# Storing the weight sums of the seven-product down projection ahead of time, and redistributing additions, query units and output tiles, in an fp32 attention-plus-GLU layer

## The chip, the cores and the metric

The kernel runs on one core of one Trainium2 chip. The metric is the device time of one execution in microseconds (us); three runs give the median. A profiled execution of the same program gives the rows that are read below. PE is the matrix engine, DVE the vector engine, ACT the scalar engine, POOL is GpSimd, and SP is the engine that issues nearly all transfers.

## The reference

Everything is fp32. With S = 2048 tokens, D = 512, 32 heads of 16 and F = 1376:

```python
xn = layernorm(x)
q, k, v = split(xn @ wqkv)                        # 32 heads of 16
phi(t) = [softmax(t @ w_phi), softmax(-t @ w_phi)]  # 32 features of a head
num = phi(q) @ (phi(k).T @ v);  den = phi(q) @ sum(phi(k)) + 1e-6
s = (num / den) @ wo
gate, up = xn @ W_gate, xn @ W_up                 # 512 -> 1376
g = silu((gate * (gate > 0) * up) @ W_down)       # 1376 -> 512
out = x + s * g
```

## The kernel before

An fp32 product is made of three passes on PE: each operand is split into a high part (a copy on ACT, rounded) and a low part (value minus high part, a subtraction on POOL or DVE), and `mm3` adds low times high, high times low and high times high in one PSUM tile. A pass of 128x128 weights over 512 columns is the unit of PE's work. In the names of tiles, an ending h or l (`wth`, `wtl`, `hh`, `hl`) is the high or low part.

The program has three stretches. First come the normalisation, the keys, values and queries, the state `phi(k).T v`, and the splitting of the GLU's weights, which are written back to DRAM (`wspill`, the names `ws` in the trace). Then the GLU runs twice over its eleven blocks `f` of 128 hidden units: the first half for tokens 0 to 1023 (blocks 0 and 1 of 512 tokens), the second half for tokens 1024 to 2047. In each `f`, `gate_up` multiplies gate and up weights (`wa`, `wb`, `wc`, `wd`) by column sets of the normalised tokens in a seven-product form; its PSUM tiles are `pa`, `pb`, `pc`, `pd`, and DVE adds them up (`pb<-pb,t`, `t<-pd,t`, `r<-pd,r` and so on).

In the second half the down projection has a seven-product form too, called turned: the first eight blocks form two groups (`GROUPS`), and each group needs seven products in the order `ORDER = (5, 3, 1, 6, 7, 2, 4)`. Product `i` has a weight operand `AW[i]` (tiles `wth`, `wtl`) and a token operand `OPS[i]`. Of the weight operands 1, 2 and 4 are plain quarters of the group's down weights (`rd`); 5, 6, 3 and 7 are sums of quarters (`ds`). `weights()` makes all seven while the second half runs: a sum, a high part, a low part each. `operand_parts()` makes the token operands by subtractions such as `t<-t,t` and `e<-t,e`. A helper `sooner()` puts each such addition on DVE or POOL, whichever the planner believes free first. `turned_down(g)` issues the products in PSUM tiles `py`, interleaved with `gate_up` at the steps `STEPS_AT`; DVE adds them to `y`.

The queries are worked off in eight units (`UNITS`), of two 256-token pieces each, by `q_pair(u)` and `q_back(u)`: DVE transposes (`pq<-pql`), takes maxima and minima (`mx<-pq`), subtracts (`eq<-pq,mx`), ACT exponentiates, POOL weighs (`ez<-eq,zB`) and normalises (`eq<-eq,qs`), DVE sums (`qs<-eq`, `qs<-ez`) and transposes (`ez<-eq`), PE makes `pnum`, ACT copies it out (`eq<-pnum`), SP stores it. Units 0 to 2 belong to the first half of the GLU and units 3 to 7 to the second.

An output tile of 128 tokens is `s` times `g` plus `x`: `out_tile` multiplies by `wo` (PSUM `pso`, 12 passes), DVE multiplies by the gate, and `sx<-yk,sx` adds `x`. Tokens 1024 to 2047 that fall to `TURNED_Q` use `out_turned`, which transposes back on DVE (`z<-y`) and adds `x` as `z<-z,sx`, half on POOL and half on DVE.

Every engine executes its instructions in program order. That order is partly written out, and partly set by a planner, `Clock`: work that is not on PE's path is held in generators, each step of which names an engine and tiles; `pump()` issues a step when the planner's estimate says that the tiles are there and the engine is at most `LIMIT` ahead (for queries times a factor), and `finish()` forces a generator to its end. The estimates are costs in the code, not measurements. All instructions go through one helper, so that the trace names line 74 for nearly all.

Of the kernel before, what the change touches and what calls it, by code (L numbers as in the profile page):

```python
# [54 lines left out]
SLACK = 3000  # L55
# [119 lines left out]
def layer_kernel(ctx: ExitStack, tc: tile.TileContext, x, wkT, wqT, wv, wo, wf, cst, out):  # L175
# [31 lines left out]
    def f32(t):  # L207
        return t.bitcast(F32)
# [369 lines left out]
    def f_prep(f, keep=True):  # L578


        rg, rd, tab = RAW.pop(f)
        b11, b12, b21, b22 = (rg[c][:, :, s, :] for c in range(2) for s in range(2))
        ta, tb = tab or two("tab", True)
        yield "gpsimd", b22
        add(nc.gpsimd, tb[:, 0], b12, b11, ALU.subtract)
        add(nc.gpsimd, ta[:, 1], b22, b12, ALU.subtract)
        if keep:
            wa, wb = w_pair("wa"), None
        else:
# [36 lines left out]
        put(f, 6, wd)  # L626
        yield from sums_of(ordered(fd[1]), plain(rd), ordered(f32(fd[0])), ALU.subtract, fd[0])
        if f not in IN_GROUP:
            put(f, 8, fd[1])
        if keep:  # L630
            FT[f], WD[f] = [wa, wb, wc, wd], fd
            nxt = f + 1
            while nxt in AHEAD:
                nxt += 1
            del rg, rd, ta, tb, tab
            if nxt < NF and nxt not in RAW:
                f_load(nxt)
        DONE.add(f)
        yield None,
# [69 lines left out]
            WQ.clear()  # L709
        yield  # L710

    RD, MADE = {}, set()

    def halves(t):
        return t.rearrange("p k (a n c) -> p n (k a) c", a=4, n=2)

    def sooner():
        ends = {k: max(pace.free[k], pace.now) + pace.FIXED[k] + pace.RATE[k] * BT for k in ("vector", "gpsimd")}
        return nc.vector if ends["vector"] < ends["gpsimd"] - SLACK else nc.gpsimd

    def d_load(g):
        RD[g] = [u4((P, 2, D), "rd") for h in range(2)]
        for m, f in enumerate(GROUPS[g]):
            nc.sync.dma_start(RD[g][m // 2][:, m % 2, :], wf[f][:, 1024:])

    def weights():

        for g in range(len(GROUPS)):
            d_load(g)
            a11, a21, a12, a22 = (halves(t)[:, x] for t in RD.pop(g) for x in range(2))  # L730
            t = {1: a11, 2: a12, 4: a22}
            for i in ORDER:
                while len(AW) > DEEP:
                    yield 2,
                src = t.pop(i, None)
                if src is None:
                    src = u2((P, 8, 64), "ds")
                    yield "vector", a11, a22
                    add(sooner(), src, *{5: (a21, a22, ALU.add), 7: (a11, a21, ALU.subtract),
                                          3: (a12, t.get(6), ALU.subtract)}[i])  # L740
                AW[i] = [u2((P, 2, 8, 32), f"wt{x}", F32R) for x in "hl"]
                yield "scalar", src
                hi, lo = (t.rearrange("p t k j -> p k t j") for t in AW[i])
                src_ = src.rearrange("p k (t j) -> p k t j", t=2)
                nc.scalar.activation(hi, src_, AF.Copy)
                yield "vector", hi
                add(sooner(), lo, src_, f32(hi), ALU.subtract)
                src_ = hi = lo = None
                MADE.add((g, i))
                if i == 5:  # L750
                    yield "vector", AW[i][1]
                    add(sooner(), src, src, a11, ALU.subtract)
                    t[6] = src
                if i == 7:
                    a11 = a21 = None
            src = a11 = a21 = a12 = a22 = None
        yield None,

    def f_reload(f, part):
# [133 lines left out]
    HS, Y, LATE = {}, {}, []  # L893
    B = {}
    OPS, AW, READY = {}, {}, set()
    queries = operands = making = None

    def raised(f, h1):
        g, block, k = IN_GROUP[f]
# [6 lines left out]
    def operand_parts():  # L906
# [16 lines left out]
        for g in range(len(GROUPS)):  # L923
            for i in ORDER:
                ops, ts = [], []
                for k in range(2):
                    while (g, *needs[i], k) not in B:
                        yield 1,
                    t, a, b = made(g, i, k)
                    if a is not None:  # L930
                        yield "sync", a, b
                        yield "gpsimd", a, b
                        add(sooner(), t, a, b, ALU.subtract)
                    ts.append(t)
                    t = a = b = None
                while len(OPS) > 1:
                    yield 1,
                for k in range(2):
# [9 lines left out]
                    add(sooner(), lo, t, f32(hi), ALU.subtract)  # L948
                    ops.append((hi, lo))
                    del t, hi, lo  # L950
                if i in drops:
# [9 lines left out]
    def turned_down(g):  # L961
# [7 lines left out]
        held = {}  # L969
        for i in ORDER:  # L970
            pace.finish(operands, lambda: (g, i) in READY)
            pace.finish(making, lambda: (g, i) in MADE)
            for t in range(2):
                c = {5: "y", 3: "y", 2: "z"}.get(i, "x"), t
                first = c not in held
                if first:
                    held[c] = ps(name="py")
                p = held[c]
                wh, wl = AW[i]
                mm3(p, lambda k: [x[:, t, 4 * k:4 * k + 4].rearrange("p a j -> p (a j)") for x in (wh, wl)],  # L980
                    lambda k: OPS[i][k], range(2), first)
                del wh, wl
                if t == 1:
# [60 lines left out]
    def q_pair(u):  # L1044
# [34 lines left out]
        late = parts[0][0] in QUERIES[1]  # L1079

        def normalize(j):
            (nc.gpsimd if late else nc.vector).tensor_tensor(
# [103 lines left out]
        yield None,  # L1186

    OHL, OF, SX, YK, LOADED = {}, {}, {}, {}, set()
    yspill = {t: dram((P, D), f"yk{t}") for t in (6, 7)}

    def o_load_turned(n):
        qs = TURNED_Q[n]
# [35 lines left out]
    def out_turned(n, d, w):  # L1228
# [25 lines left out]
    def last_turned():  # L1254
# [28 lines left out]
                nc.scalar.activation(y, y, AF.Silu)  # L1283
        for f in REST_F:
            HS.pop(f), WD.pop(f)
        q = QUERIES[1][-1]
        for n in range(2):
            for d in range(4):
                if n == 1 and d == 1:
                    o_split(q)  # L1290
                out_turned(n, d, WO)
                pace.pump()
                if n == 0 and d == 0:
                    o_split_turned(1)
                if n == 0 and d == 2:
                    o_load(q)
# [467 lines left out]
    def all_queries(half):  # L1764
# [35 lines left out]
    for half in range(2):  # L1800
# [7 lines left out]
        for f in range(NF):  # L1808
# [11 lines left out]
            if f == NF - 1:  # L1820
                if half:
                    o_load_turned(0)
                else:
                    drain()
                    pace.finish(queries)
# [36 lines left out]
        for j, b in enumerate((b1, b0)):  # L1862
            j = 1 - j
            if b == b0:
                for q in QUERIES[half][:2]:
                    o_split(q)
            parts = {}
# [21 lines left out]
        for m, q in enumerate(qs):  # L1889
            if m == 1:  # L1890
                f_reload(1, 0)
            if m + 2 < len(qs):
                o_split(qs[m + 2])
            if m + 4 < len(qs):
# [60 lines left out]
```

## Time and profile before

| what | value |
|---|---|
| median of three runs | 544.26 us (544.08 to 544.73) |
| profiled execution | 544.09 us, span 542.3 us, clock 0.996 |
| PE | 533.2 us busy, 98% of the span, 3162 matmuls |
| DVE | 403.4 us, 74% |
| ACT | 261.1 us, 48% |
| POOL | 398.8 us, 74% |
| transfers | 119.69 MB, mean 221 GB/s |

The profiled execution is 1.79 us longer than its span: what lies around the span. PE is nearly always busy, so the questions are where it stands still, and what lies behind its last matmul. The rows name a tile by the program's name without its number; `x6` in a row of the timeline means six instructions of the same form grouped in one row, and the bracket at its end gives the engine's idle time ahead of the row and what ended it.

### The profile page before, as it was taken

The page shows a single profiled execution, that of the slowest core. Times are in us where ns is not written, and L with a number is a line of the kernel's source. Part 1 is how long each engine was busy: PE and PEld are TensorE (multiplying, and loading weights), DVE is VectorE, ACT ScalarE, POOL GpSimd, SP SyncE. Part 2 cuts the span into 40 slices and gives each one's busy share as a digit, 9 for nine tenths or more (in the row PEclk, how much of TensorE's full clock was granted, in tenths as well). Part 3 has the DMA queues.
Part 4 walks back from the last instruction along what each step waited for, and adds up shares of the span by engine and source line. Part 5 has one row for each costly group of instructions (what it writes and reads, how often), then busy time and mean ns, then how long its engine had stood idle before and what let it go on. Part 6 is the DMA issues. An engine that isn't in the chain of part 4 may idle for free. (4 is left out here: it accounts for less than half of the span.)

```text
span 542.3 us, 9145 instructions
## 1 busy us (share of the span) xinstructions
PE 533.2 (98%) x3162; PEld 435.8 (80%) x3162; DVE 403.4 (74%) x629; ACT 261.1 (48%) x467; POOL 398.8 (74%) x343
## 2 busy tenths in 40 slices
PE   9999999999999999999999999999999999999995
PEld 8898887888887888787888888887787878778784
DVE  5988777687867328789983342899979999799365
ACT  3788757654425565545443250323655452643500
POOL 0669999767788999899896235446799859966652
PEclk9999999999999999999999999999999999999998
DMA  8439789557899646775879996793455456653564
GB/s 271 161 128 331 168 219 241 126 124 184 218 246 354 232 171 222 250 265 216 290 256 342 410 414 266 259 370 108 142 176 196 129 174 215 188 164 95 173 202 131
DMA packets 81166, 119.69 MB, mean 221 GB/s; under 512 B 6880, under 2 KB 39520, under 8 KB 80224
## 3 DMA queue, kind: packets, MB, share of 16 engines
q1 hardware_dynamic: 78960, 111.70, 61.1%
q0 software_dynamic: 2016, 7.34, 7.9%
q8 instruction: 25, 0.41, 0.3%
q14 instruction: 21, 0.17, 0.1%
q10 hardware_dynamic: 144, 0.07, 0.0%
HBM read 66.39 MB, written 48.50 MB: 212 GB/s over the span
## 5 line engine op out<-in xcount | busy, mean ns | idle before, releaser
L74 PE MATMUL pa<-XT,wa 128*128 128x512 f32 x264 | 67.4, 390 | 0.0
L74 DVE TENSOR_TENSOR y<-py,y 128x512 f32<-128x512 f32 x60 | 40.9, 683 | 29.4 <-PE py L74 29.4
L74 PEld LDWEIGHTS pa<-XT,wa 128*128 128x128 f32 x264 | 49.4, 188 | 11.0 <-issue 0.8
L74 POOL TENSOR_TENSOR ez<-eq,zB 128x1024 f32<-128x1024 f32 x16 | 38.4, 2408 | 6.4 <-ACT eq L74 6.4
L74 POOL TENSOR_TENSOR hl<-t,hh 128x512 fp32r<-128x512 f32 x20 | 25.9, 1297 | 15.7 <-ACT hh L74 13.8
L74 PE MATMUL pd<-XT,wd 128*128 128x512 f32 x132 | 33.8, 391 | 0.8 <-DVE t L74 0.7
L74 PE MATMUL py<-fdh,hl 128*128 128x512 f32 x88 | 34.4, 390 | 0.0
L74 PE MATMUL py<-fdl,hh 128*128 128x512 f32 x88 | 34.3, 389 | 0.0
L74 PE MATMUL py<-fdh,hh 128*128 128x512 f32 x88 | 34.2, 389 | 0.0
L74 PE MATMUL pd<-XT,wc 128*128 128x512 f32 x132 | 34.1, 391 | 0.0
L74 PE MATMUL pb<-XT,wb 128*128 128x512 f32 x132 | 33.9, 391 | 0.0
L74 PE MATMUL pc<-XT,wb 128*128 128x512 f32 x132 | 33.8, 390 | 0.0
L74 POOL TENSOR_TENSOR ol<-of,oh 128x512 fp32r<-128x512 f32 (+1 forms) x13 | 19.8, 1548 | 16.9 <-ACT oh L74 13.1
L74 PE MATMUL pq<-XT,wqh 128*128 128x512 f32 (+1 forms) x112 | 30.7, 360 | 0.0
L74 DVE TENSOR_REDUCE mx<-pk 128x32 f32<-128x512 f32 x32 | 20.5, 681 | 13.3 <-PE pk L74 13.3
L74 PE MATMUL pk<-wkh,XT 128*128 128x512 f32 x88 | 30.2, 395 | 0.0
L74 PEld LDWEIGHTS pd<-XT,wd 128*128 128x128 f32 x132 | 24.6, 188 | 6.7 <-DVE t L74 1.6
L74 PEld LDWEIGHTS pb<-XT,wb 128*128 128x128 f32 x132 | 24.6, 188 | 5.9 <-ACT wc L74 0.4
L74 PEld LDWEIGHTS pd<-XT,wc 128*128 128x128 f32 x132 | 24.6, 188 | 5.8 <-issue 0.8
L74 PEld LDWEIGHTS pc<-XT,wb 128*128 128x128 f32 x132 | 24.7, 188 | 5.5 <-issue 0.4
L74 ACT ACTIVATE hh<-t 128x512 fp32r<-128x512 f32 x21 | 13.0, 627 | 30.7 <-DVE t L74 25.6
L74 PE MATMUL pb<-XT,wc 128*128 128x512 f32 x102 | 26.0, 391 | 0.5 <-DVE pb L74 0.5
(252 smaller groups left out, 1607.0 us busy)
## 6 DMA issues: line engine op xcount, KB each, us to landing
xts<-XT SPq DMA_DIRECT2D x4, 1792.0 KB
zacc<-ek POOLq DMA_DIRECT2D x14, 512.0 KB, 5.6
XT<-xts SPq DMA_DIRECT2D x7, 1024.0 KB
rawg<-wf SPq DMA_DIRECT2D x22, 256.0 KB
ws<-wa SPq DMA_DIRECT2D x22, 256.0 KB
ws<-wb SPq DMA_DIRECT2D x22, 256.0 KB
ws<-wc SPq DMA_DIRECT2D x22, 256.0 KB
wa<-ws SPq DMA_DIRECT2D x22, 256.0 KB
```

Of the source, the lines that this page charges most:

```text
L74: return self.tc.keep_in_program_order(op(*a, **k))
```

## The change

- `weight_sums()` is new. It starts with the second query group of the first half's output tiles, makes the four sums of both groups on POOL (`ds`), splits them (`dth` on ACT, `dtl` on POOL), and stores both parts in DRAM (`WDT`). `weights()` makes nothing any more: it fetches the sums from `WDT`, and the plain operands 1, 2, 4 as slices from `wspill`, whose parts 7 and 8 are now stored for all blocks instead of three.
- `sooner()` is gone: the remaining operand additions are always POOL's.
- The `x` addition of the turned tiles is DVE's, but for one half of the first four.
- Unit 3 of the queries moves to the first half (`Q_UNITS`); from unit 3 on the planner's factor for DVE is 0.7, where it was 1.5 from unit 4 on.
- The output tiles of query piece 2 (tokens 512 to 767, tiles 4 and 5) move from the first half's end to the program's end, so that four tiles come last instead of two.
- `d_load(0)` is issued at the last block of the first half; the first half's queries are finished ahead of block 0's last down products, where it was before the last gate and up products.

```diff
-QUERIES = [(0, 1, 2), (6, 7, 4, 5, 3)]
+QUERIES = [(0, 1), (6, 7, 4, 5, 2, 3)]
+Q_UNITS = ((0, 4), (4, 8))
+PLAIN = {1: (0, 0), 2: (0, 1), 4: (1, 1)}
...
-        if f not in IN_GROUP:
-            put(f, 7, fd[0])
+        put(f, 7, fd[0])
...
+    def weight_sums():
+        for g in range(len(GROUPS)):
...
+            t = u2((P, 8, 64), "ds")
+            for i in (5, 6, 3, 7):
...
+                yield "gpsimd", a, b
+                add(nc.gpsimd, t, a, b, op)
+                parts = [u2((P, 2, 8, 32), f"dt{x}", F32R) for x in "hl"]
...
+                yield "scalar", t
+                nc.scalar.activation(hi, src, AF.Copy)
+                yield "gpsimd", hi
+                add(nc.gpsimd, lo, src, f32(hi), ALU.subtract)
+                def put(parts=parts, g=g, i=i):
+                    for x, d in zip(parts, WDT[g, i]):
+                        nc.sync.dma_start(d, f32(x).rearrange("p t k j -> p (t k j)"))
...
     def weights():
...
-                add(sooner(), lo, src_, f32(hi), ALU.subtract)
+                if i in PLAIN:
+                    n, m = PLAIN[i]
+                    AW[i] = [u2((P, 2, 2, P), f"wt{x}", F32R) for x in "hl"]
+                    for k in range(2):
+                        for x, w in enumerate(AW[i]):
+                            nc.sync.dma_start(f32(w[:, k]).rearrange("p t c -> p (t c)"),
+                                              wspill[GROUPS[g][2 * m + k]][7 + x][:, 256 * n:256 * n + 256])
+                else:
+                    yield "sync", *WDT[g, i]
+                    AW[i] = [u2((P, 2, 8, 32), f"wt{x}", F32R) for x in "hl"]
+                    for w, d in zip(AW[i], WDT[g, i]):
+                        nc.sync.dma_start(f32(w).rearrange("p t k j -> p (t k j)"), d)
...
-                        add(sooner(), t, a, b, ALU.subtract)
+                        add(nc.gpsimd, t, a, b, ALU.subtract)
...
-                    add((nc.gpsimd, nc.vector)[h], part, part, SX[n][2 * i + h])
+                    add(nc.vector if n or h else nc.gpsimd, part, part, SX[n][2 * i + h])
...
-        for j in range(2):
-            out_tile(2 * q + j, WO)
-            pace.pump()
+        for q in rest:
+            for j in range(2):
+                out_tile(2 * q + j, WO)
+                pace.pump()
...
-            if parts[0][0] in QUERIES[half]:
-                if u > 3:
-                    yield "limit", (1.5, 1)
+            if u in range(*Q_UNITS[half]):
+                if u > 2:
+                    yield "limit", (0.7, 1)
                 yield from q_pair(u)
```

PE's own order is the same but for two things: the eight `pnum` stand at other places, and the two output tiles (24 passes) stand at the end. The other engines' orders change most in the second half. Three places follow; first the kernel before, then the changed one.

DVE in the second half, where `gate_up` of the fourth and fifth blocks runs. `pb<-pb,t` is the addition that PE's next `pb` products wait for; `qs`, `qr` belong to the queries, `wtl` is a weight operand's low part. Before:

```order
L74 STREAM_TRANSPOSE ez<-eq 128x512
L74 TENSOR_REDUCE qs<-eq 128x64 x2
L74 TENSOR_TENSOR wtl<-ds,wth 128x8x2x32
L74 RECIPROCAL qr<-qs 128x128
L74 TENSOR_REDUCE qs<-ez 128x64
L74 TENSOR_TENSOR wtl<-rd,wth 128x8x2x32
L74 TENSOR_TENSOR pb<-pb,t_4368 128x512
L74 TENSOR_REDUCE qs<-ez 128x64
```

After:

```order
L75 TENSOR_TENSOR r<-pd,r 128x512
L75 TENSOR_REDUCE qs<-eq 128x64 x2
L75 TENSOR_TENSOR pb<-pb,t_4465 128x512
L75 RECIPROCAL qr<-qs 128x128
L75 TENSOR_REDUCE qs<-ez 128x64
L75 TENSOR_TENSOR t_4465<-pd,t_4465 128x512
L75 TENSOR_REDUCE qs<-ez 128x64
L75 SCALAR_TENSOR_TENSOR t_4465<-pb,t_4465 128x512
```

Both low parts have left DVE's order; between `r` and the next `pb` now stand two query sums, where a sum, a reciprocal, a third sum and the two low parts stood besides.

POOL from the first half's output tiles (`ol`, `sx`) into the second half. Before:

```order
L74 TENSOR_TENSOR ol<-of,oh 128x1024 x3
L74 TENSOR_TENSOR sx<-y,sx 128x512 x6
L74 TENSOR_TENSOR ez<-eq,zB 128x1024 x2
L74 TENSOR_TENSOR t_4098<-e_3958,u_3939 128x512
L74 TENSOR_TENSOR t_4112<-e_4049,u_4031 128x512
L74 TENSOR_TENSOR ds<-rd 128x512
L74 TENSOR_TENSOR hl<-t_4098,hh 128x512
L74 TENSOR_TENSOR hl<-t_4112,hh 128x512
L74 TENSOR_TENSOR ds<-ds,rd 128x512
```

After:

```order
L75 TENSOR_TENSOR ol<-of,oh 128x1024 x2
L75 TENSOR_TENSOR sx<-y,sx 128x512 x4
L75 TENSOR_TENSOR ds<-rd 128x512
L75 TENSOR_TENSOR dtl<-ds,dth 128x8x2x32
L75 TENSOR_TENSOR ds<-ds,rd 128x512
L75 TENSOR_TENSOR ez<-eq,zB 128x1024
L75 TENSOR_TENSOR dtl<-ds,dth 128x8x2x32
L75 TENSOR_TENSOR ds<-rd,ds 128x512
L75 TENSOR_TENSOR ez<-eq,zB 128x1024
L75 TENSOR_TENSOR dtl<-ds,dth 128x8x2x32
L75 TENSOR_TENSOR ds<-rd 128x512
L75 TENSOR_TENSOR t_4188<-e_4026,u_4007 128x512
```

The first group's sums now stand ahead of the first operand subtraction `t<-e,u`; their low parts wait for ACT's `dth`.

The program's end, first DVE, then SP. `yk` is an output tile times its gate, `z` a turned tile's. DVE before:

```order
L74 TENSOR_TENSOR z<-z,sx 128x512
L74 STREAM_TRANSPOSE z<-y 128x8x32
L74 TENSOR_TENSOR z<-z,sx 128x512
L74 TENSOR_TENSOR yk<-pso,yk 128x512
L74 TENSOR_TENSOR sx<-yk,sx 128x512
L74 TENSOR_TENSOR yk<-pso,yk 128x4x64
L74 TENSOR_TENSOR sx<-yk,sx 128x256
L74 TENSOR_TENSOR yk<-pso,yk 128x4x64
L74 TENSOR_TENSOR sx<-yk,sx 128x256
```

DVE after:

```order
L75 TENSOR_TENSOR z<-z,sx 128x512 x2
L75 STREAM_TRANSPOSE z<-y 128x8x32
L75 TENSOR_TENSOR z<-z,sx 128x512 x2
L75 TENSOR_TENSOR yk<-pso,yk 128x512 x2
L75 TENSOR_TENSOR sx<-yk,sx 128x512
L75 TENSOR_TENSOR yk<-pso,yk 128x512
L75 TENSOR_TENSOR sx<-yk,sx 128x512
L75 TENSOR_TENSOR yk<-pso,yk 128x4x64
L75 TENSOR_TENSOR sx<-yk,sx 128x256
L75 TENSOR_TENSOR yk<-pso,yk 128x4x64
L75 TENSOR_TENSOR sx<-yk,sx 128x256
```

SP before:

```order
L74 DMA of<-od_5586 128x1024
L74 DMA yk<-yk_167 128x512
L74 DMA yk<-yk_168 128x512
L74 DMA sx<-x 128x512 x2
L74 DMA out<-z 32x8x128 x16
L74 DMA out<-sx 128x512
L74 DMA out<-sx 128x256 x2
```

SP after:

```order
L75 DMA yk<-yk_186 128x512
L75 DMA sx<-x 128x512 x2
L75 DMA out<-z 32x8x128 x4
L75 DMA sx<-x 128x512 x2
L75 DMA out<-z 32x8x128 x12
L75 DMA out<-sx 128x512 x3
L75 DMA out<-sx 128x256 x2
```

Between the last store of a turned tile (`out<-z`) and the last store of all now lie four output tiles on PE instead of two.

More of the change, by code (lines that the diff above doesn't have):

```diff
@@ L710, in q_tile @@
         yield
-    RD, MADE = {}, set()
+    RD, MADE, SUMMED, PUTS = {}, set(), set(), {}
     def halves(t):
         return t.rearrange("p k (a n c) -> p n (k a) c", a=4, n=2)
-    def sooner():
-        ends = {k: max(pace.free[k], pace.now) + pace.FIXED[k] + pace.RATE[k] * BT for k in ("vector", "gpsimd")}
-        return nc.vector if ends["vector"] < ends["gpsimd"] - SLACK else nc.gpsimd
     def d_load(g):
@@ L724, in d_load @@
             nc.sync.dma_start(RD[g][m // 2][:, m % 2, :], wf[f][:, 1024:])
+    WDT = {(g, i): [dram((P, 512), f"wdt{g}{i}{x}") for x in "hl"] for g in range(len(GROUPS)) for i in (5, 6, 3, 7)}
+    def weight_sums():
+        for g in range(len(GROUPS)):
+            if g not in RD:
+                yield 100,
+                d_load(g)
+            a11, a21, a12, a22 = (halves(t)[:, x] for t in RD.pop(g) for x in range(2))
+            yield 40,
+            yield "sync", a11, a22
+            t = u2((P, 8, 64), "ds")
+            for i in (5, 6, 3, 7):
+                a, b, op = {5: (a21, a22, ALU.add), 6: (t, a11, ALU.subtract), 3: (a12, t, ALU.subtract),
+                            7: (a11, a21, ALU.subtract)}[i]
+                yield "gpsimd", a, b
+                add(nc.gpsimd, t, a, b, op)
+                parts = [u2((P, 2, 8, 32), f"dt{x}", F32R) for x in "hl"]
+                hi, lo = (x.rearrange("p t k j -> p k t j") for x in parts)
+                src = t.rearrange("p k (t j) -> p k t j", t=2)
+                yield "sync", t
+                yield "scalar", t
[5 more added lines that the diff above has]
+                        nc.sync.dma_start(d, f32(x).rearrange("p t k j -> p (t k j)"))
+                    SUMMED.add((g, i))
+                PUTS[g, i] = pace.when(parts[1], put)
+                del parts, hi, lo, src, a, b, put
+            del t, a11, a21, a12, a22
+        yield None,
@@ L726, in weights @@
     def weights():
         for g in range(len(GROUPS)):
-            d_load(g)
-            a11, a21, a12, a22 = (halves(t)[:, x] for t in RD.pop(g) for x in range(2))
-            t = {1: a11, 2: a12, 4: a22}
             for i in ORDER:
-                while len(AW) > DEEP:
+                while len(AW) > DEEP or i not in PLAIN and (g, i) not in SUMMED:
                     yield 2,
[L735 to L746, printed above, removed]
-                add(sooner(), lo, src_, f32(hi), ALU.subtract)
-                src_ = hi = lo = None
-                MADE.add((g, i))
[L750 to L755, printed above, removed]
@@ L895, in layer_kernel @@
     OPS, AW, READY = {}, {}, set()
-    queries = operands = making = None
+    queries = operands = making = sums = None
     def raised(f, h1):
@@ L971, in turned_down @@
             pace.finish(operands, lambda: (g, i) in READY)
+            if i not in PLAIN:
+                pace.finish(sums, lambda: (g, i) in PUTS)
+                pace.finish(PUTS[g, i])
             pace.finish(making, lambda: (g, i) in MADE)
@@ L979, in turned_down @@
                 wh, wl = AW[i]
-                mm3(p, lambda k: [x[:, t, 4 * k:4 * k + 4].rearrange("p a j -> p (a j)") for x in (wh, wl)],
+                mm3(p, lambda k: [x[:, k, t] if i in PLAIN else x[:, t, 4 * k:4 * k + 4].rearrange("p a j -> p (a j)")
+                                  for x in (wh, wl)],
                     lambda k: OPS[i][k], range(2), first)
@@ L1077, in total @@
             nc.vector.tensor_reduce(sums[:, s, j, :], src, op=ALU.add, axis=AX.X)
-        late = parts[0][0] in QUERIES[1]
+        late = u > 2
         def normalize(j):
@@ L1824, in layer_kernel @@
                     drain()
-                    pace.finish(queries)
+                    d_load(0)
                     for q in QUERIES[0][:4]:
@@ L1864, in layer_kernel @@
             if b == b0:
+                pace.finish(queries)
+                pace.finish(BACK[Q_UNITS[0][1] - 1])
                 for q in QUERIES[half][:2]:
@@ L1891, in layer_kernel @@
                 f_reload(1, 0)
+                sums = pace.add(weight_sums())
             if m + 2 < len(qs):
```

18 lines of the change are left out of this document (8 added, 10 removed).

## The prediction

> **What bounds the kernel now.** I read four views in this order: the page's engine line, the waits of PE, the work by stretches, and the timeline around each place where PE stood still. The page says that PE is the bound:
>
> ```profile
> PE 533.2 (98%) x3162; PEld 435.8 (80%) x3162; DVE 403.4 (74%) x629; ACT 261.1 (48%) x467; POOL 398.8 (74%) x343
> ```
>
> The change takes no matmul from PE, so it can only win where PE stands still or after its last product. The stretches (start:end, then busy us and count of PE, PEld, DVE, ACT and POOL, then clock, DMA share, GB/s) tell which engine is near its limit beside PE:
>
> ```profile
> 282.00:342.00 60.00, 60.00 (x293) 49.07 (x292) 22.19 (x33) 18.11 (x29) 29.11 (x24) 1.00 0.89 342
> 342.00:471.50 129.50, 127.73 (x641) 102.91 (x639) 119.11 (x163) 59.69 (x99) 96.88 (x63) 1.00 0.59 196
> 471.50:513.00 41.50, 41.32 (x234) 32.38 (x233) 31.89 (x50) 20.08 (x33) 27.14 (x19) 1.00 0.51 157
> ```
>
> DVE is 37% busy in the first half's end, 92% in the body of the second half (119.11 of 129.5), 77% after it. PE loses nothing in the first of these, and its losses fall in the other two. These are the five places, each as the row before the stop and the row after it (the bracket is idle time by a modelled end, so I take starts instead):
>
> ```profile
> 374.14 1.52 PE L74 MATMUL pd<-XT,wc 128*128 128x512 f32 x6
> 376.20 1.65 PE L74 MATMUL pb<-XT,wc 128*128 128x512 f32 x6 [0.53 <-DVE pb L74]
> ...
> 384.93 0.96 PE L74 MATMUL pc<-XT,wb 128*128 128x512 f32 x3
> 386.46 0.47 PE L74 MATMUL py<-XT,wtl 128*128 128x512 f32 x1 [0.58 <-ACT eq L74]
> ...
> 439.28 0.39 PE L74 MATMUL py<-hh,wth 128*128 128x512 f32 x1
> 440.33 1.66 PE L74 MATMUL pd<-XT,wd 128*128 128x512 f32 x6 [0.66 <-DVE t L74]
> ...
> 471.41 0.39 PE L74 MATMUL py<-hh,wth 128*128 128x512 f32 x1
> 471.93 1.67 PE L74 MATMUL pd<-XT,wd 128*128 128x512 f32 x6
> ...
> 480.26 1.52 PE L74 MATMUL pa<-XT,wa 128*128 128x512 f32 x6
> 481.83 0.50 PE L74 MATMUL py<-XT,wtl 128*128 128x512 f32 x1
> ```
>
> Undisturbed, six passes take 1.36 us from start to start (three products of 0.39 us that follow each other at 439.28 and before it start 0.227 apart). So the stops are 376.20 - 374.14 - 1.36 = 0.70; at 386.46, three passes and a slow start of 0.11 after 384.93, 0.74; 440.33 - 439.28 - 0.227 = 0.82; 471.93 - 471.41 - 0.227 = 0.29; 481.83 - 480.26 - 1.36 = 0.21: together 2.76. After each, the first group lasts about 0.11 longer (1.65 against 1.52): 0.55 more. **PE loses 3.31 us in the second half to late operands.** What DVE did just then:
>
> ```profile
> 374.85 0.68 DVE L74 TENSOR_TENSOR eq<-mx,pq 128x512 f32<-128x512 f32 x1
> 375.45 0.69 DVE L74 TENSOR_TENSOR pb<-pb,t 128x512 f32<-128x512 f32 x1
> ...
> 385.62 0.70 DVE L74 TENSOR_TENSOR wtl<-ds,wth 128x512 fp32r<-128x512 f32 x1
> ...
> 439.61 0.67 DVE L74 TENSOR_TENSOR t<-pd,t 128x512 f32<-128x512 f32 x1
> ...
> 469.50 1.78 DVE L74 TENSOR_TENSOR wtl<-rd,wth 128x512 fp32r<-128x512 f32 x1
> 471.20 0.68 DVE L74 TENSOR_TENSOR t<-pd,t 128x512 f32<-128x512 f32 x1
> ```
>
> Each time the operand that PE needs stood in DVE's queue behind something else. At 376.20 it is a query's subtraction, at 471.93 a weight operand of 1.78 us. At 386.46 the profile names ACT, yet the product reads the low part that DVE finished at 386.32, 0.14 us earlier: both were late. At 440.33 no weight work stands ahead, only queries: taking the weight sums alone would not mend that one directly, but the thinner queue may.
>
> The second loss is behind PE's last product:
>
> ```profile
> 532.18 3.50 POOL L74 TENSOR_TENSOR z<-z,sx 128x512 f32<-128x512 f32 x2 [4.88 <-DVE z L74]
> ...
> 534.00 3.95 SPq L74 DMA_DIRECT2D out<-z  x8
> 535.16 1.08 DVE L74 TENSOR_TENSOR sx<-yk,sx 128x512 f32<-128x512 f32 x1
> 536.20 0.28 PE L74 MATMUL pso<-woh,oh 128*128 128x256 f32 x1
> 536.60 0.42 DVE L74 TENSOR_TENSOR sx<-yk,sx 128x256 f32<-128x256 f32 x1
> 537.39 0.43 DVE L74 TENSOR_TENSOR sx<-yk,sx 128x256 f32<-128x256 f32 x1
> 538.05 1.42 SPq L74 DMA_DIRECT2D out<-sx  x3
> ```
>
> SP spends 534.00 to 537.95 issuing eight stores of turned tiles, about 0.49 us apiece, and only then the three of the last tiles, though DVE had the first of them at 536.24. The last is issued about 0.95 us after 538.05, at 539.0, and the span ends at 542.3: 3.3 us from the last issue to the end.
>
> **The change part by part.** Weight sums and low parts, removed from DVE, and a query unit moved (mean ns of one in the groups by shape):
>
> ```profile
> L74 DVE TENSOR_TENSOR wtl<-rd,wth 128x512 fp32r<-128x512 f32 x5 | 7.8, 1566 | 0.1
> L74 DVE TENSOR_TENSOR wtl<-ds,wth 128x512 fp32r<-128x512 f32 x5 | 5.7, 1140 | 0.3
> L74 DVE TENSOR_TENSOR ds<-rd 128x512 f32<-128x512 f32 x3 | 3.9, 1299 | 0.0
> L74 DVE TENSOR_TENSOR ds<-rd,ds 128x512 f32<-128x512 f32 x1 | 2.4, 2410 | 0.8 <-POOL ds L74 0.8
> L74 DVE TENSOR_TENSOR y<-py,y 128x512 f32<-128x512 f32 x60 | 40.9, 683 | 29.4 <-PE py L74 29.4
> L74 POOL TENSOR_TENSOR hl<-t,hh 128x512 fp32r<-128x512 f32 x20 | 25.9, 1297 | 15.7 <-ACT hh L74 13.8 <-DMA pql<-pq 1.8
> L74 DVE STREAM_TRANSPOSE ez<-eq 128x512 f32<-128x512 f32 x32 | 21.2, 686 | 0.1
> L74 DVE TENSOR_REDUCE mx<-pq 128x32 f32<-128x512 f32 x32 | 20.5, 681 | 0.4
> L74 DVE TENSOR_REDUCE qs<-eq 128x64 f32<-128x1024 f32 x16 | 19.1, 1204 | 0.0
> L74 DVE TENSOR_REDUCE qs<-ez 128x64 f32<-128x1024 f32 x16 | 18.9, 1190 | 0.7 <-POOL ez L74 0.7
> ```
>
> The fourteen weight additions on DVE took 7.8 + 5.7 + 3.9 + 2.4 = 19.8 us, all of them in the body of the second half. One of eight query units is at least (21.2 + 20.5 + 19.1 + 18.9) / 8 = 10.0 us by these four groups alone. Without 29.8 us the body has 89.3 us of DVE in 129.5, 69%. That is under the 77% of the stretch after it, where the two smallest stops fall (0.29 + 0.11 and 0.21 + 0.11, 0.72 in all). I take the row nearest to the new load: the stops shrink from 3.31 to 0.7, because queries still stand between `gate_up`'s additions (two sums of 1.2 us ahead of a `pb`, in the listing of the change). The ends are 0 and 3.31: the tighter planner factor can spread the queries so that none is left, or they bunch as they did at 440.33. Gain: 2.6.
>
> DVE's additions with two SBUF inputs (`wtl`, `ds`) take 1.1 to 2.4 us, those that read PSUM (`y`) 0.68, and POOL takes 1.30 for the same shape. The Trainium skill, GPSIMD Engine Reference, section 3.1, has an addition on GpSimd 1.96 times as long as on DVE and keeps to DVE for elementwise work. The trace agrees with that only against the 0.68; against `wtl` and `ds` POOL is no slower. By the page's ratio the move would load POOL with more time than DVE loses, which the rivals take up as a wait; by the rows it is an even exchange.
>
> There were 8 sums and 14 low parts, 14 of these 22 on DVE and 8 on POOL. The six low parts of plain operands vanish, and the other 16 additions are all POOL's: 8 more x 1.30 = 10.4 us. POOL had 96.88 + 27.14 = 124.0 us in the 171 us from 342 to 513; 134.4 would be 79%, before the moved unit's operations are taken off, and the first sums stand right behind the first half's output tiles, where POOL was 49% busy (29.11 of 60). Cost: 0 for PE, covered by that slack; if the cover is gone, the price is that of the third rival.
>
> Transfers: sixteen more stores of 256 KB (parts 7 and 8), sixteen stores and sixteen loads of sums, 24 slices of 128 KB, two gate tiles out and back: about 17 MB, some 9 MB of them in the 129.5 us of the body, 70 GB/s on top of 196. The stretch before ran at 342 GB/s with PE never idle, so I price them at 0. They are 77 more issue rows on SP at about 0.49 us, 38 us over the whole program. Behind a store that waits for POOL's low part stand the next block's weight loads; a wait of a microsecond or two is covered, since they are issued a block ahead of use. Its bounds are 0 and one stop like the largest, 0.93. I take 0.
>
> Unit 3 in the first half: the 10.0 us of DVE and more go where DVE was busy 22.2 of 60 us; PE lost nothing there. The earlier `finish` puts query work ahead of the last down products' additions. Bounds 0 and 0.93; I take 0. The two output tiles move 24 passes, 24 x 0.227 = 5.4 us, from one place on PE to another: 0.
>
> The end: the eight stores of turned tiles now lie four output tiles, 48 x 0.227 = 10.9 us, ahead of PE's end, and SP is free when DVE finishes. DVE's 535.16 row took 1.08 beside the second of POOL's additions, which run to 535.68; alone it should be near 0.68, so that the last pair starts right behind PE's last product: 536.55 + 0.41 + 0.43, about 537.4, issue at 537.45, end 3.3 later at 540.75. Gain 1.55 of 542.3. Ends: 0, if SP is still held, and 1.8.
>
> Sum for the profiled execution: 544.09 - 2.6 - 1.55 = 539.9. The median stands 0.17 above it, so 540.1.
>
> **The rivals.** First, stops remain. Queries stood ahead at 376.20 and 440.33, 1.5 of the 2.76, and four of the second half's five units stay there; a new late operand can replace each old one. Then only the end is won: 544.26 - 1.55 = 542.7. Against it speaks the 23 points of load that DVE loses (92 to 69%). Second, the end is not won: the stores of four tiles' rows queue as before, and only the stops go: 544.26 - 2.6 = 541.7. Against it: ten microseconds of PE lie between. Third, on the slower side: POOL makes every turned operand late. It now makes each sum, each low part and each operand difference in one queue, with `ez<-eq,zB` and the like between. With fourteen products late by x, the time is 539.4 + 14 (x + 0.11); above x = 0.31 it is slower than 545.35. At the 0.58 that PE idled at 386.46 it would be 549.1. For it: POOL's 79%; against: no wait of PE for POOL is among the five. Fourth, all stops go: 539.4. Fifth, the change does little: SP's extra issues delay a block's loads and each of four or five is worth 0.93, which brings back what was won: 543.8 to 544.7.
>
> **How the numbers follow.** A difference under 0.2%, 1.1 us, can't be told from no change here. Chances: forecast with the fourth, 539.0 to 541.2: 0.62, of which 0.05 still lower; first rival 0.15; second 0.10; third 0.08; fifth 0.05. Faster, under 543.2: 0.62 + 0.15 + 0.10 less 0.02 for a first rival with an end half won: 0.85; same 0.07; slower 0.08. The range runs from 539.0 to 542.8, which leaves the third and the fifth and a little below it.
>
> **What would show it.** Right: no row of PE with a wait on DVE longer than 0.3 us after 342; no DVE `wtl` or `ds`; the last `out<-sx` issued within 0.2 us of DVE's end, and 4.5 us from PE's last start to the span's end, where it was 6.1. Wrong: PE waits on POOL or on ACT behind `dth`, on a transfer of `wth` or `wa`, or the five stops still there at other tiles.

## The result and the profile after

The changed kernel takes 540.95 us (median of four runs, 540.86 to 541.09) against 544.20 us of the kernel before in the same comparison: a ratio of 0.9939, 95% interval 0.9921 to 0.9956. The forecast was 540.1, in a range from 539.0 to 542.8. The profiled execution has a span of 539.2 us at clock 1.0.

The page's engine line, and the three stretches that the prediction showed (start:end, then busy us and count of PE, PEld, DVE, ACT, POOL, then clock, DMA share, GB/s), of the kernel after:

```profile
PE 532.7 (99%) x3162; PEld 436.3 (81%) x3162; DVE 381.0 (71%) x614; ACT 258.7 (48%) x462; POOL 403.9 (75%) x353
```

```profile
282.00:342.00 60.00, 59.19 (x312) 47.10 (x311) 37.47 (x57) 21.86 (x33) 34.63 (x26) 1.00 0.97 367
342.00:471.50 129.50, 129.50 (x653) 105.36 (x652) 96.61 (x146) 56.18 (x93) 106.73 (x75) 1.00 0.83 288
471.50:513.00 41.50, 41.50 (x211) 33.75 (x210) 17.74 (x29) 17.42 (x31) 19.98 (x15) 1.00 0.50 159
```

In the body of the second half PE is now busy for all 129.50 us, where it was 127.73, and for all of the stretch after it: the five stops are gone, none of them replaced. DVE has gone from 119.11 to 96.61 us there. But the first stretch, in which PE had lost nothing, now has 59.19 of 60. PE's waits say with what (for whom: us in total, times, longest):

```profile
PE pidle L75 <- DVE mhalf L75: 1.1, 1, 1.1
PE pnum L75 <- DVE ez L75: 0.8, 1, 0.8
PE pk L75 <- ACT pk L75: 0.2, 1, 0.2
```

The first and the last stand in the kernel before as well, at the program's start. The middle one is new, and the timeline of PE, DVE and POOL around it shows its place:

```profile
315.65 0.39 PE L75 MATMUL py<-fdh,hh 128*128 128x512 f32 x1
315.97 0.66 PE L75 MATMUL pnum<-ez,kvt 64*32 64x256 f32 x16
317.44 1.25 PE L75 MATMUL pnum<-ez,kvt 64*32 64x256 f32 x16 [0.81 <-DVE ez L75]
318.61 0.50 PE L75 MATMUL py<-fdh,hl 128*128 128x512 f32 x1
...
311.32 1.94 POOL L75 TENSOR_TENSOR eq<-eq,qs 128x1024 f32<-128x1024 f32 x1
...
312.68 2.05 DVE L75 TENSOR_TENSOR y<-py,y 128x512 f32<-128x512 f32 x3 [2.13 <-PE py L75]
316.07 0.69 DVE L75 TENSOR_TENSOR y<-py,y 128x512 f32<-128x512 f32 x1 [1.35 <-PE py L75]
316.68 1.29 DVE L75 STREAM_TRANSPOSE ez<-eq 128x512 f32<-128x512 f32 x2
```

Unit 3's second pair of transposes needs POOL's normalisation, which ended at 313.26. DVE then idled for 1.35 us, up to 316.07, for the fourth addition of the down products, and only behind that stood the transposes. PE went from the last down product (315.65) straight to the first half of `pnum` and then stood in front of its second half. From `pnum`'s start at 315.97 to the next product's at 318.61 are 2.64 us; where nothing waits it is 1.03 (383.90 to 384.93 in the kernel before): 1.6 us lost.

The end of the kernel after:

```profile
534.59 0.28 PE L75 MATMUL pso<-woh,oh 128*128 128x256 f32 x1
535.36 0.42 DVE L75 TENSOR_TENSOR sx<-yk,sx 128x256 f32<-128x256 f32 x1
530.44 5.71 SPq L75 DMA_DIRECT2D out<-sx  x5
```

SP issues the last three of its five stores with pauses between them, each 0.03 us after the addition that it stores: the last at 535.82, where DVE ended at 535.79. In the kernel before the last was issued at 539.05, 1.23 us after DVE's end at 537.82. From PE's last start to the span's end are 539.2 - 534.59 = 4.6 us, where it was 6.1. So 544.09 - 3.3 (stops) - 1.5 (end) + 1.6 (new stop) = 540.9, the profiled execution's time (539.2 and 1.8 around it).

### The profile page after: what moved, and what is told of

The parts are those of the page before. It is cut to its first block, busy times and chain, and to the rows that moved or that the text cites. A ratio compares the mean times of both kernels' runs of the same rounds, so it can differ in the third digit from the quotient of the medians.

```text
span 539.2 us, 9274 instructions
## 1 busy us (share of the span) xinstructions
PE 532.7 (99%) x3162; PEld 436.3 (81%) x3162; DVE 381.0 (71%) x614; ACT 258.7 (48%) x462; POOL 403.9 (75%) x353
## 4 chain that ended last, share of the span: by engine, by line
PE 85%; POOL 5%; ACT 4%; DVE 3%; issue 2%; POOLq 0%; DVEq 0%; ACTq 0%
PE py L75 21%; PE pd L75 12%; PE pa L75 12%; PE pb L75 10%; PE pso L75 8%; PE pc L75 7%; PE pk L75 6%; PE pq L75 3%; PE pv L75 2%; PE pnum L75 2%; POOL XT L75 1%; PE pkv L75 1%; POOL t L75 1%; ACT junk L75 1%; PE pidle L75 1%
## 5 line engine op out<-in xcount | busy, mean ns | idle before, releaser
L75 POOL TENSOR_TENSOR hl<-t,hh 128x512 fp32r<-128x512 f32 x21 | 27.1, 1297 | 13.2 <-ACT hh L75 10.9
L75 DVE TENSOR_TENSOR pb<-pb,t 128x512 f32<-128x512 f32 x17 | 11.9, 699 | 28.7 <-ACT pd L75 28.5
L75 ACT ACTIVATE pb<-pa 128x512 f32<-128x512 f32 x17 | 9.9, 583 | 33.6 <-PE pa L75 33.5
```

Source lines behind the costliest of these rows:

```text
L75: return self.tc.keep_in_program_order(op(*a, **k))
```

## The experiments

All were compared with the kernel before on the same chip; its medians were 544.3 to 544.6. Ratios are to it. Every run but e2, e5 and e11 contains the edit of e1; e9, e12 and e13 also finish the first half's queries where the changed kernel does.

| run | what | us | ratio (95%) |
|---|---|---|---|
| e1 | changed, transposes ahead of the addition | 539.54 | 0.9910 (0.9897 to 0.9923) |
| e2 | changed, unit 3 late again | 546.20 | 1.0028 (1.0017 to 1.0039) |
| e3 | e1, factor 1.5 | 539.55 | 0.9908 (0.9893 to 0.9922) |
| e4 | e1, sums made late | 542.00 | 0.9962 (0.9949 to 0.9976) |
| e5 | changed, unit 3 late, factor 1.5 | 539.72 | 0.9904 (0.9890 to 0.9919) |
| e6 | e1, turned `x` addition shared | 539.68 | 0.9905 (0.9890 to 0.9920) |
| e7 | e1, two tiles last | 540.26 | 0.9914 (0.9900 to 0.9928) |
| e9 | before, the end alone | 542.60 | 0.9964 (0.9951 to 0.9976) |
| e10 | e4, weight additions on POOL | 539.40 | 0.9904 (0.9890 to 0.9918) |
| e11 | e5, operand additions on either | 540.25 | 0.9918 (0.9905 to 0.9932) |
| e12 | before, all additions on POOL and the end | 566.11 | 1.0402 (1.0387 to 1.0417) |
| e13 | e12, planner's POOL cost 1.9 | 562.17 | 1.0333 (1.0311 to 1.0356) |

**e1: the new stop.**

```diff
+                if b == b1 and i == TPB - 1:
+                    u = Q_UNITS[0][1] - 1
+                    pace.finish(queries)
+                    pace.finish(BACK[u], lambda: DONE_Q[u] >= 2)
                 y_sum(b, i, parts[i], False, True)
```

> The changed kernel with one swap on DVE: the last two transposes of query unit 3 (ez<-eq) stand ahead of the fourth addition of block 1's last down products (y<-py) instead of behind it; every other engine's order is the same. Theory: the changed kernel's new stop on PE (the pnum products at 316 to 318 us, about 1.65 us beyond what pnum costs elsewhere) comes from that order alone. Then the stop shrinks to 0.2 us or less and the time is 539.3 (539.1 to 539.6). Rival: the transposes' input comes late from POOL (eq<-eq,qs), so the stop stays or moves to the addition: 540.5 to 541.0.

The stop is gone: PE has no wait after the start of the program, and the span is 537.7, 1.5 shorter. One exchange of neighbours on DVE was the whole of it; the input from POOL was there in time.

**e2, e3, e5: unit 3 and the planner's factor.** e2 changes `Q_UNITS` to `((0, 3), (3, 8))`, e3 the factor to 1.5 in e1, and e5 both, with 1.5 from unit 4 on as before.

> The changed kernel with query unit 3 back in the second half (units 0 to 2 first, 3 to 7 second), all else as changed. The stop at 316 us must go, since unit 2's pnum is done long before. Theory A: the weight sums' leaving was enough, the second half keeps running without a stop: 539.3. Theory B: unit 3's 17 us of DVE work were what crowded the second half: stops of 1 to 2 us come back there: 540.3 to 541.3.

> The changed kernel with the swap of e1 and the planner's factor for the queries at 1.5 as before instead of 0.7. Theory A: with 30% less work on DVE the factor does nothing: 539.3. Theory B: queries bunch ahead of gate_up's additions again, as at 440.33 in the kernel before: one to three stops of 0.3 to 0.9: 539.8 to 541.3.

> The changed kernel with both of the query edits undone: unit 3 in the second half and the planner's factor 1.5 from unit 4 on; sums stored and fetched, four tiles last. In the run with unit 3 late and factor 0.7 the last unit was behind at the end (8 us of stops at 507 to 517); with 1.5 it should be in time. Theory A: the weight work on DVE was what made PE wait, and the query edits were not needed: no stop over 0.3 us in the second half, 539.4 (539.1 to 539.9). Theory B: the queries need them: stops of 1 to 2 us, 540.4 to 541.5. Theory C: the last unit is late again whatever the factor: 544 to 546.

e3 and e5 went as theory A has it: with the one query edit undone (e3) or both (e5) the second half has no stop over 0.2 us. e2 was expected by neither theory. Its body has no stop, but with one unit more and the tight factor the last unit was not through when its output was wanted, and PE stood in front of `pnum` among the output tiles (timeline of PE, then two stretches):

```profile
507.02 0.39 PE L75 MATMUL pso<-oh,woh 128*128 128x512 f32 x1
509.39 1.25 PE L75 MATMUL pnum<-ez,kvt 64*32 64x256 f32 x16 [1.98 <-DVE ez L75]
511.96 1.69 PE L75 MATMUL pnum<-ez,kvt 64*32 64x256 f32 x16 [1.32 <-DVE ez L75]
514.17 0.63 PE L75 MATMUL pso<-ol,woh 128*128 128x512 f32 x1
```

```profile
507.00:513.00 6.00, 2.70 (x32) 0.71 (x32) 4.67 (x9) 0.00 (x0) 1.26 (x2) 0.84 0.17 48
513.00:518.00 5.00, 5.00 (x25) 3.48 (x12) 0.84 (x3) 2.24 (x4) 0.00 (x0) 0.50 0.90 297
```

So the factor 0.7 costs the queries their lead, and unit 3's move pays for that: with both edits undone (e5) the time is that of e1, which has both, and 1.2 us less than the changed kernel's, which has both and the new stop.

**e4, e10, e11: which additions, and on which engine.** e4 is e1 with `weights()` of the kernel before, `sooner()` included; e10 is e4 with POOL throughout, in the additions and in what the planner waits for:

```diff
-                    add(sooner(), src, ...)
+                    add(nc.gpsimd, src, ...)
...
-                add(sooner(), lo, src_, f32(hi), ALU.subtract)
+                add(nc.gpsimd, lo, src_, f32(hi), ALU.subtract)
```

e11 is e5 with `sooner()` for the token operands' additions.

> The changed kernel with the swap of e1, but all seven weight operands made in the second half as before (sums and low parts on DVE or POOL as the planner chooses; nothing of them stored or fetched). Theory A: the weight work on DVE is what made PE wait: stops of 1 to 2.5 us come back: 540.3 to 541.8. Theory B: the queries made it, and unit 3's move with the factor 0.7 would have been enough: 539.3 to 539.6.

> The kernel with the sums made late (e4), but every weight sum and low part on POOL instead of where the planner chooses: nothing stored or fetched, DVE free of the weight work as in the changed kernel; POOL makes 22 additions (1.3 us each) in the second half instead of 16, none of them ahead of it. Theory A: it is only DVE's queue that had to be cleared, storing and fetching buys nothing: no stop in the second half, 539.4 (539.2 to 539.9). Theory B: POOL, in the second half alone, brings the operands late or ACT's copies wait for it ahead of PE's evictions: stops of 1 us and more, 540.4 to 543.

> The kernel with both query edits undone (e5; sums stored, four tiles last), and with the token operands' additions where the planner chooses, DVE or POOL, as before, instead of always POOL. Theory A: the weight sums alone were the cause; the operands' few additions on DVE cost nothing: 539.4 to 539.9. Theory B: their 1.1 to 1.8 us apiece on DVE bring back one or two stops of 0.3 to 0.9: 540.0 to 541.3.

e4 lost 2.0 us in one stop and 0.8 in smaller ones and slow restarts: theory A, though its 542.0 lies 0.2 above that theory's range. The stop shows a way of which the prediction had not thought (timeline of e4: DVE, ACT, PE):

```profile
366.01 2.41 DVE L76 TENSOR_TENSOR ds<-rd,ds 128x512 f32<-128x512 f32 x1 [1.40 <-POOL ds L76]
...
368.46 0.63 ACT L76 ACTIVATE wth<-ds 128x512 fp32r<-128x512 f32 x1 [5.81 <-DVE ds L76]
369.00 0.58 ACT L76 ACTIVATE pb<-pa 128x512 f32<-128x512 f32 x1
...
366.25 1.52 PE L76 MATMUL pc<-XT,wb 128*128 128x512 f32 x6
369.63 0.73 PE L76 MATMUL pb<-XT,wb 128*128 128x512 f32 x2 [1.85 <-ACT pb L76]
```

DVE's sum waits for one of POOL's, then takes 2.41 us, most of them beside another POOL instruction (`eq<-eq,qs`, 365.94 to 367.88); ACT's copy waits for it; and ACT's next instruction is `pb<-pa`, which PE needs. A weight sum that nobody wants for several microseconds holds PE through two queues in order. e10 differs from e4 in the engine alone and has no such stop: 539.40, as good as e1, with no split weight operand fetched (124.9 MB moved instead of 136.5; the parts 7 and 8 are still stored for all blocks, unread). Making the sums early and storing them was not what won. e11 came out between its theories: the time lies in the range of theory B, but its two stops are only 0.21 and 0.24 us with their slow starts; its interval overlaps with e5's, so that the time alone can't tell them apart.

The body of the second half by busy time (columns as above) shows that DVE's load does not tell the stops. First e4, then e11:

```profile
342.00:471.50 129.50, 127.51 (x641) 102.95 (x640) 115.75 (x160) 59.29 (x100) 100.77 (x66) 1.00 0.58 198
```

```profile
342.00:471.50 129.50, 129.50 (x677) 104.16 (x676) 115.04 (x169) 58.28 (x98) 111.46 (x74) 1.00 0.85 289
```

With 115.75 us of DVE e4 loses 2.8 us of PE by starts, with 115.04 e11 loses 0.5.

**e6, e7, e9: the end.** e6 shares the `x` addition of the turned tiles as before; e7 goes back to two tiles last (`QUERIES` of the kernel before, `rest` of one piece); e9 is the kernel before with the four tiles and that addition.

> The kernel of e1 with the x addition of the turned tiles shared as before (first half of each pair on POOL, second on DVE). Theory A: these additions now lie ten microseconds ahead of the end, so who makes them is worth nothing: 539.4, and 4.6 us from PE's last start to the span's end. Theory B: sharing the port makes DVE's last additions late again: 0.4 to 1.5 us more, 539.8 to 541.0.

> The kernel of e1 with two output tiles last as before (tiles 4 and 5 back at the first half's end; the planner places some query work elsewhere by it), the x addition of the turned tiles on DVE as changed. Theory A: the stores of the turned tiles hold SP again at the end: from PE's last start to the span's end 6.1 us as before instead of 4.6, the time 541.0. Theory B: DVE's additions alone bring the stores early enough: 4.6 to 5.2 us, 539.4 to 540.1.

> The kernel before with the end alone changed: four output tiles last, x addition of the turned tiles on DVE; weight sums, operand additions, query units and factor as before. Theory A: the two gains are independent: PE's stops in the second half stay at about 3.3 us and the end gains 1.5: 544.4 - 1.5 = 542.9 (542.5 to 543.3). Theory B: with two output tiles fewer between the halves the queries' order shifts and the stops change by more than 0.5: outside this.

From PE's last start to the span's end: e6 4.6 us, e7 5.6, the changed kernel 4.6, before 6.1. With two tiles last SP is still issuing the turned tiles' stores when DVE has the first of the last tiles (SP of e7):

```profile
530.44 3.96 SPq L75 DMA_DIRECT2D out<-z  x8
534.49 1.42 SPq L75 DMA_DIRECT2D out<-sx  x3
```

So of the 1.5 us the four tiles bring 1.0 beyond DVE's additions, which by themselves bring 0.5, and with the four tiles DVE's additions bring nothing (e6). e7's 540.26 lies between its theories. e9 keeps the five stops of the kernel before (0.71, 0.73, 0.83, 0.29 and 0.26 us by starts, each within 0.05 of what it was), and its end is 4.15 us: the two gains are independent, theory A, with 0.4 more at the end than expected.

**e12, e13: the two together, without the query edits.** e12 is e9 with every `add(sooner(), ...)` on POOL; e13 adds one line in the second half:

```diff
+                pace.RATE = {**pace.RATE, "gpsimd": 1.9}
```

> The kernel before with two edits only: the end as changed (four output tiles last, x addition of the turned tiles on DVE), and every weight and operand addition of the turned products on POOL, made in the second half; no stored sums, no moved query unit, factor 1.5. Theory A: which engine makes these additions is all that the stops hung on, the stored sums and the query edits bring nothing: 539.4 (539.1 to 540.0). Theory B: with five query units and 22 weight additions POOL is too full in the second half (about 150 of 175 us), or the queries still stop PE: 540.3 to 543.

> The kernel of e12, which lost 22 us in two stops at 489 and 520 us where the last two query units' pnum waited, with one number changed from the second half on: the planner's cost of a POOL element, 5.0 to 1.9 ns (with its fixed 340 ns that is 1.31 us for 512 elements, where the trace has 1.29 to 1.31; before it believed 2.9). Theory A: the queries were late because the planner believed POOL full and held their POOL steps back: now they are issued in time, the two stops go, and at most some 0.3 to 0.9 us stops come back where queries now stand closer together on DVE: 539.4 to 541.5. Theory B: POOL is really too full in the second half (22 weight additions, the operands and five units): the wait moves to other places, the time stays above 544.

By theory A e12 would have been the smallest change that wins everything; it loses 22 us, outside the ranges of both theories. Its body has no stop. But the last two query units were not through at the end, and PE stood for 10 and 11 us in front of their `pnum` (POOL, DVE and PE of e12):

```profile
492.04 4.93 POOL L76 TENSOR_TENSOR ol<-of,oh 128x512 fp32r<-128x512 f32 x4 [3.42 <-ACT oh L76]
496.94 3.82 POOL L76 TENSOR_TENSOR eq<-eq,qs 128x1024 f32<-128x1024 f32 x2
...
498.90 1.30 DVE L76 STREAM_TRANSPOSE ez<-eq 128x512 f32<-128x512 f32 x2 [3.37 <-POOL eq L76]
...
499.67 1.69 PE L76 MATMUL pnum<-ez,kvt 64*32 64x256 f32 x16 [9.97 <-DVE ez L76]
```

e13 gives the planner a cost for POOL near the measured one. The two stops at the end go, as theory A has it, and stops of 4.6, 1.4, 3.1, 2.5 and 6.6 us come between 371 and 475 us instead (read in the longest of its executions, 566.4 us): the median stays at 562, theory B. What the planner issues sooner then waits for POOL in DVE's and ACT's queues, ahead of `gate_up`'s additions. The longest of them (POOL and DVE of e13):

```profile
466.28 2.55 POOL L76 TENSOR_TENSOR XT<-t,XT 128x512 fp32r<-128x512 f32 x2
468.77 2.50 POOL L76 TENSOR_TENSOR t<-t,t 128x512 f32<-128x512 f32 x2
471.21 1.28 POOL L76 TENSOR_TENSOR ds<-rd 128x512 f32<-128x512 f32 x1
...
467.95 4.62 DVE L76 SCALAR_TENSOR_TENSOR qd<-qs 128x64 f32<-128x64 f32 x1
474.00 0.68 DVE L76 TENSOR_TENSOR t<-pd,t 128x512 f32<-128x512 f32 x1
```

An instruction that takes 0.23 us where POOL is idle (303.83 in the changed kernel) took 4.62, to 0.08 us after the end of POOL's run without a gap at 472.49, and `t<-pd,t`, for which PE waited, stood behind it. The other seven of this form in e13 took 0.57 to 1.28 us. One of them (DVE, then POOL):

```profile
386.98 1.02 DVE L76 SCALAR_TENSOR_TENSOR qd<-qs 128x64 f32<-128x64 f32 x1
...
385.36 2.55 POOL L76 TENSOR_TENSOR hl<-u,hh 128x512 fp32r<-128x512 f32 x2 [0.93 <-PE pa L76]
387.87 2.54 POOL L76 TENSOR_TENSOR t<-t,t 128x512 f32<-128x512 f32 x2
```

It ended at 388.00, 0.09 us after the end of one POOL instruction (387.91), though POOL's next one followed at once.

e10 (22 weight additions on POOL from 361 us on, unit 3 early, factor 0.7) and e5 (16, the first eight of them before 358 us, unit 3 late) run without a stop over 0.2 us; e12 has neither relief. POOL's busy time in the body does not tell them apart: 110.5 us in e10, 111.7 in e5, 111.8 in e12. How full POOL may be is not settled more closely than that, nor which of the reliefs does it: the runs between were not made.

## Why the prediction was right or wrong

**The stops.** The mechanism held: late operands in DVE's queue, 3.3 us, and they left with the additions, as e10 against e4 shows. The size was off. The forecast kept 0.7 us, the loss of the stretch whose DVE load was nearest, 77% beside an expected 69%. None was left. The load came out at 75% (96.61 of 129.5 us), and e11 against e4 shows that the load is the wrong measure. What counts is what stands in order ahead of the one operand that PE waits for; in e4 that was a long addition that itself waited. The remark that no weight work stood ahead at 440.33 was true, and that stop left too: e5 has the same queries, with the factor of before, and none of the stops.

**The end** came out at 1.5 as forecast (1.55), and for the reasons given: the last store's issue follows DVE's end by 0.03 us instead of 1.23, and DVE's end follows PE's last start by 1.20 instead of 1.62. e7 shows the larger part to be the four tiles'.

**Unit 3 in the first half** is the step that failed. The prediction had seen that the earlier `finish` puts query work next to the last down products, set its bounds at 0 and 0.93, and took 0, because DVE was only 37% busy there. It measured 1.6, outside the bounds. DVE was idle when it mattered; the transposes stood behind an addition that waited for PE, and PE waited for the transposes. The bound came from the largest stop of the trace before, but a stop of this kind has the length of a chain, PE's product, an addition, two transposes. Without it the kernel takes 539.54 (e1), near the fourth rival's 539.4.

**POOL** cost nothing in the changed kernel, and the third rival did not come. A crowded POOL can cost: e12 and e13 take 1.04 and 1.03 times the time before, though what is late there is the queries' and `gate_up`'s work, not the turned operands. The prediction put the load at 79% and took the slack as cover; after, it is 106.73 + 19.98 = 126.7 of 171, 74%. e5 and e10 have 135.1 and 135.2 us there, the 79%, and no stop over 0.2 us, so the cover held at that figure too. Of the sixteen additions for the stored sums only the first ran before 342 (at 340.1); the others ran from 344 to 426, so that the slack of the first half's end, which the prediction named, was hardly used.

The prediction read DVE's 1.1 to 2.4 us for an addition as its cost, and the move to POOL at 1.30 as an even exchange. That reading was wrong: much of DVE's time was waiting for POOL. In the kernel before (DVE, then POOL):

```profile
462.62 0.68 DVE L74 TENSOR_TENSOR wtl<-rd,wth 128x512 fp32r<-128x512 f32 x1
...
459.16 2.99 POOL L74 TENSOR_TENSOR t<-t,t 128x512 f32<-128x512 f32 x2
463.34 1.30 POOL L74 TENSOR_TENSOR hl<-r,hh 128x512 fp32r<-128x512 f32 x1 [1.19 <-ACT hh L74]
...
468.99 1.74 POOL L74 TENSOR_TENSOR XT<-r,XT 128x512 fp32r<-128x512 f32 x1
```

With POOL idle, from 462.15 to 463.34, a low part took 0.68 us. The one of 1.78 us at 469.50, ahead of the stop at 471.93, ended 0.55 us after the end of POOL's row of 468.99. Twelve of the fourteen weight additions on DVE ended 0.55 us after the end of a POOL instruction that was running when they began; the other two took 0.67 and 0.68. Additions that read PSUM, such as `pb<-pb,t`, took 0.68 to 0.70 beside a running POOL. By these rows some 10 of the 19.8 us were waiting (19.8 less 14 times 0.68, an estimate), and the work itself takes POOL nearly twice as long, 1.30 against 0.68, close to the ratio of 1.96 that the prediction quoted and set aside. So moving the additions took more off DVE than it put on POOL: with sixteen moved, e10 has 20.7 us less of DVE than e4 and 14.9 more of POOL.

The Trainium skill, SBUF — State Buffer, section "SBUF: two separate sides", says that a DVE instruction with two SBUF inputs and a GpSimd instruction that reads SBUF exclude each other for a whole instruction. The rows above agree, and so do seven of the eight `qd<-qs` of e13, each of which ended 0.08 or 0.09 us after the end of one POOL instruction. The eighth, of 4.62 us, goes further: it sat through the rest of one and three whole POOL instructions. Why is open.

**Transfers** at 0: right. The body moved 288 GB/s where it moved 196 (the estimate was 70 more, it is 92), and e10 with 11.6 MB fewer is no faster than e1. SP issues 76 rows more, not 77.

The misses add up: the stops gave 0.7 more than forecast and unit 3 took 1.6, net 0.9; the result is 0.85 above the forecast. That it is no further off is in part luck, since the two misses have opposite signs. The signs came as written: no wait of PE for DVE after 342, no `wtl` or `ds` on DVE, the last store 0.03 us after DVE's end, and 4.6 us behind PE's last start (4.5 forecast). For the one new stop, before 342, no sign had been named.

## What to carry to other kernels

An engine that executes in order is not judged by its load: follow, for each operand that the bounding engine waits for, what stands ahead of it in its queue and what that waits for in turn, through every queue on the way. Moving work to a second engine can win everything (e10) or lose 4% (e12), with the same instruction counts on PE, DVE and POOL, by whether the work that shares that engine still ends in time; check the last user, not the average. And when work is forced to an end at a fixed place, look at the neighbours on each engine: here the exchange of two neighbours was worth 1.4 us.

## What the runs showed of the hardware

- In e2 the granted clock fell after a pause of PE: behind some 6 us in which PE was busy for 2.70, it was 0.50 for 5 us, and passes started 0.43 us apart instead of 0.227. In these 5 us PE did the work of 2.6, so the pause cost some 2.4 us more than itself. Behind the stop of 2.0 us in e4 the clock stayed at 1.00.
- In the kernel before, a 128x512 addition on DVE with two SBUF inputs took 0.68 us beside an idle POOL; begun while POOL was running, it ended 0.55 us after the end of a POOL instruction, up to 2.41 us in all. Once, in e13, such a wait lasted through four POOL instructions: 4.62 us for an instruction of 0.23.
- From PE's last start to the span's end the kernels with four tiles last take 4.6 us where the sums are stored (the changed kernel, e1, e3, e5, e6, e11) and 4.2 where they are not (e4, e9, e10, e12, e13), though DVE's last additions are alike; e2, with stored sums, has 4.3. The difference lies behind the issue of the last store: 3.36 us from there to the span's end in the changed kernel, 2.93 in e9. The reason is open.
